# Attention by 128-token tile over all heads, woven into a SwiGLU feed-forward block

## The chip, the cores and the metric

The kernel runs on one core of one Trainium2 chip. The metric is the device time of one execution in microseconds (us). Engines are named as in the profile: PE is TensorE's matrix multiply and PEld its weight load, DVE is VectorE, ACT is ScalarE, POOL is GpSimd and SP is SyncE; POOL and SP issue the DMAs here. L12 is line 12 of the kernel that a row belongs to.

## The reference, cut to what matters

```python
batch, n_heads, seq, head_dim = (8, 8, 576, 64)          # q, k, v, float32
scores = scale * np.matmul(q, k.transpose(0, 1, 3, 2))   # scale = 1/sqrt(64)
bias = slopes[:, None, None] * (-np.abs(rel))            # rel = i - j
mask = (rel >= 0) & (rel < 128)
scores = np.where(mask, scores + bias[None], -1e9)
attn = np.exp(scores - np.max(scores, axis=-1, keepdims=True))
attn = attn / (np.sum(attn, axis=-1, keepdims=True) + 1e-09)
attn_out = np.matmul(attn, v)
x = attn_out.transpose(0, 2, 1, 3).reshape(4608, 512)    # tokens x (heads * head_dim)
g = x @ w_gate                                           # 512 x 1536
out = (g / (1 + np.exp(-g)) * (x @ w_val)) @ w_out       # 1536 x 512
```

Each query sees itself and the 127 keys before it. Both kernels compute exp(score) without the maximum and multiply by a constant table of exp(bias), which is 0 outside the window, and get the sum of the weights as a 65th column of ones beside v.

## The kernel before, in words

The kernel holds x transposed, in four fp16 tiles `xT` of 128 channels by 4608 tokens (L83). It walks through the 8 batches (L187) and in each through 4 pairs of heads (L192).

For a pair of heads, SP issues nine DMAs in rows of 256 bytes that bring q, k and v in fp32 (L199, L203). PE transposes q and k in fp32 with an identity (L216, L218), and ACT copies the results to fp16 `qT` and `kT` (L221, L222) and v to `va` (L227, L229). PE makes the scores with keys on the output partitions (L247; the two heads use the upper and the lower 64 rows of the array), ACT applies Exp (L255 to L259), and DVE multiplies by the table (L264 to L267). The weighted sum (L279 to L285) has v as the stationary operand, so that its result has the head's 64 channels and the row of sums on the output partitions and the queries along the free axis. ACT copies the 64 rows to `avs` (L290, L291), and DVE copies the one row of sums to `cs` (L293, L295).

The division for a whole batch is in `batch_tail` (L165): two reciprocals of 128x576 (L168, L169), a matmul per head that spreads the reciprocal over 64 partitions (L176, L178), and multiplications that write `xT` (L180, L182). It is called after the first pair of heads of the next batch (L301).

The feed-forward block, `moe_block` (L125), takes 512 tokens at a time. For each of 12 column blocks of the hidden layer it runs 4 gate matmuls (`pg_`, L133) and 4 value matmuls (`pv_`, L138) of 128x512, then a Tanh on ACT (`tt`, L143) and two operations on DVE (`uu`, L145; `hT`, L148). The three PSUM banks of the tag "gv" go round. Then come 4 output tiles of 12 matmuls each (`po_`, L152) in one PSUM bank, a copy on ACT (`osb`, L156) and an output DMA from POOL (L157). There are nine such blocks and 1296 matmuls in them. A block is called at the third pair of heads of a batch (L303), and the last two after all of the attention (L312). A scheduler in the tile framework moves instructions within each engine's queue, so that attention and feed-forward matmuls come mixed around these calls; within a queue the order is then fixed.

The weights come through POOL's queue in fp32 in twelve DMAs, and ACT casts them to fp16 (L97 to L108), called after the first pair of heads.

Of the kernel before, what the change touches and what calls it, by code (L numbers as in the profile page):

```python
# [12 lines left out]
ALU = mybir.AluOpType  # L14


@with_exitstack
def kernel(
# [10 lines left out]
    nc = tc.nc  # L29

# [3 lines left out]
    WIN = 128  # L34
    P = 128

    NQT = (S + P - 1) // P
    LAST = S - (NQT - 1) * P
    HP = H // 2
    NKB = DM // P  # L40
    NMB = DFF // P
    NNB = NTOK // 512
    BCOL = 512

    slopes = [2.0 ** (-8.0 * (hh + 1) / H) for hh in range(H)]

    jj = np.arange(P)[:, None]
    ii = np.arange(P)[None, :]
    bconst = np.zeros((P, H, 2, P), dtype=np.float32)
    for hh in range(H):  # L50
        for dq in range(2):
            u = ii - jj + 128 * dq
            valid = (u >= 0) & (u < WIN)
            bconst[:, hh, dq, :] = np.where(valid, np.exp(-slopes[hh] * u), 0.0)
    b0 = bconst[:, :, 0, :]
    b1 = bconst[:, :, 1, :]
    tmask = np.concatenate([b0, b1], axis=2).astype(np.float16)
    tmask2 = np.concatenate(
        [b0, b1[:, :, 0:64], b0[:, :, 0:64]], axis=2).astype(np.float16)
    ident32 = np.eye(P, dtype=np.float32)  # L60
    ident16 = np.eye(P, dtype=np.float16)

    sel = np.zeros((P, 4, 64), dtype=np.float16)
    for j in range(4):
        sel[32 * j, j, :] = 1.0

    tmask_d = nc.inline_tensor(tmask, name="tmask")
    tmask2_d = nc.inline_tensor(tmask2, name="tmask2")
    ident32_d = nc.inline_tensor(ident32, name="ident32")
    sel_d = nc.inline_tensor(sel, name="selconst")  # L70

    consts = ctx.enter_context(tc.tile_pool(name="consts", bufs=1))
    idm = consts.tile([P, P], FP32, name="idm")
    nc.sync.dma_start(idm, ident32_d.ap())
    tm = consts.tile([P, H, 256], FP16, name="tm")
    nc.sync.dma_start(tm, tmask_d.ap())
    tm2 = consts.tile([P, H, 256], FP16, name="tm2")
    nc.sync.dma_start(tm2, tmask2_d.ap())
    selc = consts.tile([P, 4, 64], FP16, name="selc")
    nc.sync.dma_start(selc, sel_d.ap())  # L80

    xt_pool = ctx.enter_context(tc.tile_pool(name="xt", bufs=1))
    xT = [xt_pool.tile([P, NTOK], FP16, name=f"xT{pg}", tag=f"xT{pg}")  # L83
          for pg in range(NKB)]

# [259 lines left out]
```

## Time and profile before

| What | Value |
|---|---|
| Median of the 3 runs (lowest, highest) | 566.29 us (565.98, 566.87) |
| Span of the profiled execution, first to last instruction | 566.0 us |
| Mean granted TensorE clock over the span | 0.927 |
| Instructions in the span | 7238 |
| DMA packets and bytes | 120676, 48.84 MB |

The profile shows one execution. For this one the page gives the span and no time of its own beside it; the runs stand between 0.0 and 0.9 us off the span. A row of a group of instructions reads: line, engine, operation, output<-inputs, shapes, count | busy us, mean ns of one | idle time of that engine just before them and what ended it. A row of the timeline or of the chain of waits begins with its start in us and its length; a matmul's length covers its way through the array, so that the next one starts earlier than it ends. A row of the table by stretches gives, for each engine, busy us and the count of instructions, then the granted clock as a share of full speed, the DMA engines' busy share, and GB/s.

### The profile page before, as it was taken

The numbers are of one execution on the slowest core, as the hardware profiler recorded it, in microseconds if no ns is written. First come the engines' busy times: TensorE is split into PE (matmuls) and PEld (weight loads), VectorE is DVE, ScalarE is ACT, GpSimd is POOL, SyncE is SP. The second block draws the span as 40 slices with busy tenths as digits, with TensorE's granted clock in tenths as the row PEclk, the third lists the DMA queues.
The fourth block names the chain that finished last, engine by engine and source line by source line (L and its number), as shares of the span: only waits on it lengthen the run. The fifth ranks groups of instructions, "written<-read, shape, count | busy, mean of one in ns | idle before, by whom it ended". The sixth has DMA issues, their size and how long they took to land.

```text
span 566.0 us, 7238 instructions
## 1 busy us (share of the span) xinstructions
PE 469.6 (83%) x2448; PEld 237.9 (42%) x2448; DVE 366.0 (65%) x720; ACT 277.4 (49%) x669; POOL 27.3 (5%) x52
## 2 busy tenths in 40 slices
PE   1634689986999699969996999789986999599994
PEld 0322435443544355434544354445443544144441
DVE  1222778759774967497758786678758774875450
ACT  3868718352844466455645383528353844032321
POOL 1110000010001000100000000100010001000001
PEclk9999999996999699978998699969996999699998
DMA  8997614132412423142414241424131101000101
GB/s 262 309 300 212 139 28 112 41 112 67 104 44 76 104 62 86 59 102 62 104 52 107 51 106 26 122 51 100 42 101 38 43 1 57 19 2 19 57 11 63
DMA packets 120676, 48.84 MB, mean 86 GB/s; under 512 B 116032, under 2 KB 116288, under 8 KB 120640
## 3 DMA queue, kind: packets, MB, share of 16 engines
q1 hardware_dynamic: 115776, 29.51, 23.6%
q0 software_dynamic: 4864, 18.88, 9.4%
q8 instruction: 19, 0.31, 0.2%
q14 instruction: 17, 0.14, 0.1%
HBM read 38.93 MB, written 9.44 MB: 85 GB/s over the span
## 4 chain that ended last, share of the span: by engine, by line
PE 41%; issue 30%; DVE 13%; ACT 7%; DMA 7%; POOL 1%; POOLq 0%; ACTq 0%
PE pt_a L216 3%; DVE rc L168 3%; DMA wtmp<-in_moe_w_gate_dram 3%; PE bcA L176 3%; DVE cs L293 2%; DMA wtmp<-in_moe_w_val_dram 2%; PE avA L279 2%; DMA wtmp<-in_moe_w_out_dram 2%; ACT osb L156 2%; DVE ex L264 2%; DVE xT L180 1%; POOL out_dram L157 1%; DVE cs L190 1%; PE pt_b L218 1%; ACT exr L255 1%
## 5 line engine op out<-in xcount | busy, mean ns | idle before, releaser
L264 DVE TENSOR_TENSOR ex<-exr,tm 128x768 f16<-128x768 f16 x64 | 34.9, 545 | 85.0 <-ACT exr L257 84.3
L279 PE MATMUL avA<-ex,va 128*65 128x256 f16 (+1 forms) x256 | 44.7, 304 | 35.4 <-DVE ex L264 31.1
L152 PEld LDWEIGHTS <-hT 128*128 128x128 f16 x432 | 42.1, 98 | 51.5 <-issue 4.3
L138 PEld LDWEIGHTS <-wv_sb 128*128 128x128 f16 x432 | 42.5, 98 | 49.9 <-issue 4.1
L133 PEld LDWEIGHTS <-wg_sb 128*128 128x128 f16 x432 | 41.1, 99 | 52.8 <-issue 13.7
L293 DVE COPY cs<-avA 1x512 f32<-1x512 f32 x64 | 43.4, 678 | 17.5 <-ACT avs L290 16.8
L180 DVE TENSOR_TENSOR xT<-avs,bcA 64x512 f16<-64x512 f16 x64 | 43.5, 680 | 13.0 <-PE bcB L178 11.5
L279 PEld LDWEIGHTS <-va 128*65 128x65 f16 x256 | 30.6, 126 | 49.0 <-issue 37.3
L221 ACT ACTIVATE qT<-pt_a 128x512 f16<-128x512 f32 x32 | 19.1, 597 | 64.6 <-PE pt_a L216 64.6
L290 ACT CAST avs<-avA 64x512 f16<-64x512 f32 x64 | 37.0, 578 | 25.1 <-PE avB L283 23.5
L176 PE MATMUL bcA<-rc,selc 128*64 128x512 f16 x64 | 34.6, 568 | 16.4 <-DVE cs L293 5.7
L157 POOL DMA_DIRECT2D out_dram<-osb x36 | 19.5, 542 | 493.9 <-ACT kT L222 357.5
L247 PE MATMUL ps<-qT,kT 64*128 64x256 f16 (+2 forms) x320 | 31.6, 274 | 7.4 <-ACT kT L221 7.4
L255 ACT ACTIVATE exr<-ps 128x512 f16<-128x512 f32 x64 | 34.8, 598 | 6.0 <-PE ps L247 5.4
L257 ACT ACTIVATE exr<-ps 128x448 f16<-128x448 f32 x64 | 34.3, 545 | 0.0
L216 PE MATMUL pt_a<-idm,qnat 128*128 128x128 f32 x128 | 22.1, 300 | 14.6 <-DMA knat<-in_k_dram 12.7
L168 DVE RECIPROCAL rc<-cs 128x576 f16<-128x576 f32 x8 | 30.0, 3753 | 0.3
L169 DVE RECIPROCAL rc<-cs 128x576 f16<-128x576 f32 x8 | 29.9, 3738 | 0.3
L216 PE MATMUL pt_a<-idm,knat 128*128 128x128 f32 x128 | 22.9, 306 | 5.6 <-ACT qT L221 5.6
L247 PEld LDWEIGHTS <-kT 64*128 64x128 f16 (+1 forms) x320 | 15.0, 100 | 27.4 <-ACT kT L221 12.7
L216 PEld LDWEIGHTS pt_a<-idm,qnat 128*128 128x128 f32 x128 | 16.5, 152 | 19.5 <-DMA knat<-in_k_dram 12.7
L176 PEld LDWEIGHTS <-selc 128*64 128x64 f16 x64 | 9.4, 148 | 28.9 <-issue 20.9
(647 smaller groups left out, 878.2 us busy)
## 6 DMA issues: line engine op xcount, KB each, us to landing
out_dram<-osb POOLq DMA_DIRECT2D x36, 256.0 KB, 2.3
qnat<-in_q_dram SPq DMA_DIRECT2D x64, 128.0 KB, 2.7
knat<-in_k_dram SPq DMA_DIRECT2D x64, 128.0 KB, 2.9
vnat<-in_v_dram SPq DMA_DIRECT2D x64, 128.0 KB, 2.6
wtmp<-in_moe_w_gate_dram POOLq DMA_DIRECT2D x4, 768.0 KB, 6.7
wtmp<-in_moe_w_val_dram POOLq DMA_DIRECT2D x4, 768.0 KB, 6.6
wtmp<-in_moe_w_out_dram POOLq DMA_DIRECT2D x4, 768.0 KB, 6.2
tm<-tmask SPq DMA_DIRECT2D x2, 512.0 KB, 5.8
```

What stands on the lines that cost most here:

```text
L133: nc.tensor.matmul(pg_, wg_sb[:, kb, m * P:(m + 1) * P], xT[kb][:, col0:col0 + ncol], start=(kb == 0), stop=(kb == NKB - 1))
L138: nc.tensor.matmul(pv_, wv_sb[:, kb, m * P:(m + 1) * P], xT[kb][:, col0:col0 + ncol], start=(kb == 0), stop=(kb == NKB - 1))
L152: nc.tensor.matmul(po_, hT[:, m, mb * P:(mb + 1) * P], wo_sb[:, m, :], start=(m == 0), stop=(m == NMB - 1))
L168: nc.vector.reciprocal(rc[:, 0, :], cs[:, 0, :])
L176: nc.tensor.matmul(bcA, selc[:, j_, :], rc[:, g_, 0:512], start=True, stop=True)
L180: nc.vector.tensor_mul(xT[hp][hb:hb + 64, c0:c0 + 512], avs[:, 0:512], bcA)
L216: nc.tensor.transpose(pt_a[:, t * P:(t + 1) * P], src[:, t, :, :], idm)
L247: nc.tensor.matmul(pss[hh][0:kr, c0:c0 + w], kT[hb:hb + 64, kt * P:kt * P + kr], qT[hb:hb + 64, qc:qc + w], start=(si == 0), stop=(si == l ...
L255: nc.scalar.activation(exr[hh][:, 0:512], ps, AF.Exp)
L264: nc.vector.tensor_mul(ex[hh][:, 0:768], exr[hh][:, 0:768], tmr)
L279: nc.tensor.matmul(avA[:, ac:ac + w], va[:, kt, hh, :], ex[hh][:, ec:ec + w], start=(si == 0), stop=(si == 3))
L293: nc.vector.tensor_copy(cs[32 * j_:32 * j_ + 1, g_, 0:512], avA[64:65, :])
```

## The change

The attention is written anew; the arithmetic of the feed-forward block stays. Batches are taken in pairs. A pair has 9 tiles of 128 tokens: 4 of the first batch, 4 of the second, and one that holds the last 64 tokens of both. A tile with all 8 heads is a unit, and there are 36 units.

- Loads: POOL issues one DMA each for q, k and v of a tile, again in rows of 256 bytes, and the DMA casts fp32 to fp16 on its way into SBUF (L143). The weights come the same way, straight into their fp16 tiles (L344, L404), without ACT. The output DMAs move from POOL to SP (L328). SP loads four tables instead of two.
- Transposes: 8 fp16 transposes of 128x128 per tile go to one PSUM bank, and DVE copies them out (L162 to L166).
- Scores: as before with keys on the output partitions, the two heads of a pair on the two halves of the array's rows; 8 matmuls of 256 columns per unit (L209), 4 Exps of 128x512 on ACT with the scale in them (L223), 2 multiplications of 128x1024 by the table on DVE (L227).
- Weighted sum: the weights are the stationary operand and v with its column of ones the moving one (65 columns), so that queries are on the output partitions: 16 matmuls per unit (8 or 24 at the ends, L254). The sum is then a column, and the division is a reciprocal of 128x4 and a multiplication of 128x256 on DVE, twice per unit (L256, L257). `batch_tail` with its spreading matmuls, and the copies `avs` and `cs`, go.
- Since x now has tokens on partitions, 4 more transposes per unit and a copy on ACT make the feed-forward block's operand (L281, L282).
- Order: attention and feed-forward are generators. The feed-forward one yields after every 4 matmuls; a loop at the end of the program draws from both, about one step of attention for one of feed-forward, a unit being 8 steps. An output tile of block n-1 is run in three steps after each of the column blocks 1 to 4 of block n. The last four output tiles use the four banks of the attention.

In the diff, `att_step()` draws one step of the attention.

```diff
-    def batch_tail(args):
...
+    def load(rank):
...
+        for t_, src in ((tk, k), (tq, q), (tv, v)):
+            for p0, p1, b, r0 in pieces(s, c):
+                nc.gpsimd.dma_start(
+                    t_[p0:p1, :, 0:D],
+                    src[b, :, r0:r0 + p1 - p0, :].rearrange("h p d -> p h d"))
...
+        pt = ps_a.tile([P, 8, P], FP16, name="pt", tag="a")
+        for j in range(4):
+            nc.tensor.transpose(pt[:, j, :], tk[:, 2 * j:2 * j + 2, :], idm)
+        for j in range(4):
+            nc.tensor.transpose(pt[:, 4 + j, :], tq[:, 2 * j:2 * j + 2, :], idm)
+        nc.vector.tensor_copy(kTs[s][:, :, cols], pt[:, 0:4, :])
+        nc.vector.tensor_copy(qTs[s][:, :, cols], pt[:, 4:8, :])
...
+            for n, (j, w, val) in enumerate(todo):
+                nc.tensor.matmul(av[:, j, :], w, val, start=(n == 0), stop=(n == len(todo) - 1))
+            rec = xpool.tile([P, 4, 1], FP32, name="rec", tag="rec", bufs=4)
+            nc.vector.reciprocal(rec, av[:, :, D:D + 1])
+            nc.vector.tensor_mul(x[:, 4 * half:4 * half + 4, :], av[:, :, 0:D],
+                                 rec.broadcast_to([P, 4, D]))
...
+        for kb in range(NKB):
+            nc.tensor.transpose(pt[:, kb, :], x[:, kb * P:(kb + 1) * P], idm)
+        nc.scalar.copy(dst, pt)
...
+    def attention():
...
+            if i < last:
+                transposes_to(need_rank[i + 1])
+                after = scores(i + 1)
+            for n in range(4):
+                for f in after[n]:
+                    f()
+                if n == 2 and i + 2 <= last:
+                    transposes_to(need_rank[i + 2])
+                yield i
+            weighted(i)
+            yield i
+            loads_to(i + 8)
+            yield i
+            x_transposed(i)
+            yield i
+            yield i + 1
...
+    load_w(wg2, wg_sb, 0, 128)
+    load_w(wv2, wv_sb, 0, 128)
+    loads_to(3)
...
+    for a0 in (0, 6):
+        nc.gpsimd.dma_start(wo_sb[:, a0:a0 + 6, :], wo2[:, a0:a0 + 6, :])
+    loads_to(7)
...
+        target = base + step * (4.55 * 8) / per_block
+        while att_done < target and att_step():
+            att_done += 1
```

POOL's queue at the start of the program, before: `wtmp` is the fp32 buffer that ACT casts from.

```order
L340 UNCONDITIONAL_BRANCH
L101 DMA wtmp<-in_moe_w_gate_dram 128x1536
L101 DMA wtmp<-in_moe_w_val_dram 128x1536
L104 DMA wtmp<-in_moe_w_out_dram 128x3x512
L101 DMA wtmp<-in_moe_w_gate_dram 128x1536
```

The same queue at a later place of its first part, now: `kn`, `qn` and `va` are the k, q and v of a tile.

```order
L344 DMA wv_sb<-in_moe_w_val_dram 128x4x512
L140 MEMSET va 128x8
L143 DMA kn<-in_k_dram 128x8x64
L143 DMA qn<-in_q_dram 128x8x64
L143 DMA va<-in_v_dram 128x8x64
L404 DMA wo_sb<-in_moe_w_out_dram 128x6x512 x2
L140 MEMSET va 128x8
L143 DMA kn<-in_k_dram 128x8x64
```

POOL's queue held the weights alone, beside SP's with q, k and v; now all of them stand in one queue, and the tiles 6 and 7 (the last of the first eight) behind all of the weights.

PE's queue where the first feed-forward matmul stands, before, with buffer numbers: `bcA` and `bcB` spread the reciprocals of batch 0, and `pg__852` is the first gate tile.

```order
L176 LDWEIGHTS selc_64
L176 MATMUL bcA_637<-rc_116,selc_64 64x512
L178 LDWEIGHTS selc_64
L178 MATMUL bcB_638<-rc_116,selc_64 64x64
L133 LDWEIGHTS wg_sb_76
L133 MATMUL pg__852<-xT0_69,wg_sb_76 128x512
```

The same place now: `px_502` are the transposes of the fourth unit's x, and `ps_524` and `ps_525` the last scores of the sixth unit.

```order
L281 LDWEIGHTS x_470
L281 MATMUL px_502<-idm_58,x_470 128x128
...
L209 LDWEIGHTS kT_174
L209 MATMUL ps_519<-qT_173,kT_174 128x256
...
L209 MATMUL ps_524<-qT_173,kT_174 128x256
...
L209 MATMUL ps_525<-qT_173,kT_174 128x256
...
L295 LDWEIGHTS wg_sb_65
L295 MATMUL pg_509<-xT_283,wg_sb_65 128x512
```

In front of this first gate matmul now stand 64 transposes of q and k (those of tiles 0 to 7), 48 score matmuls (units 0 to 5), 56 of the weighted sum and 16 of x; behind it stand the 1296 feed-forward matmuls with 224, 272, 488 and 128 of these four kinds between them.

DVE's queue in the first feed-forward block, before:

```order
L145 SCALAR_TENSOR_TENSOR uu<-tt,pg__897 128x512
L293 COPY cs<-avA 1x512
L295 COPY cs<-avB 1x64
L293 COPY cs<-avA 1x512
L295 COPY cs<-avB 1x64
L148 TENSOR_TENSOR hT<-uu,pv__898 128x512
L145 SCALAR_TENSOR_TENSOR uu<-tt,pg__912 128x512
```

DVE's queue in a stretch of gate and value steps, now:

```order
L227 TENSOR_TENSOR ex<-exr,m_reg 128x1024 x2
L300 SCALAR_TENSOR_TENSOR uu<-tt,pg 128x512
L256 RECIPROCAL rec<-av 128x4
L310 TENSOR_TENSOR hT<-uu,pv 128x512
L257 TENSOR_TENSOR x<-av,rec 128x256
L256 RECIPROCAL rec<-av 128x4
L257 TENSOR_TENSOR x<-av,rec 128x256
L300 SCALAR_TENSOR_TENSOR uu<-tt,pg 128x512
```

Before, a head pair's copies of the sums stood between `uu` and `hT`; now a unit's reciprocals and multiplications do, and its multiplications by the table ahead of them, all through the program.

More of the change, by code (lines that the diff above doesn't have):

```diff
@@ L55 @@
[L55 to L68, printed above, removed]
@@ L80 @@
[L80 to L84, printed above, removed]
[L86 to L90 removed]
+    NSUP = B // 2
```

522 lines of the change are left out of this document (294 added, 228 removed).

## The prediction

> **What bounds the kernel now.** I read the page's busy shares first, then its chain of work that ended last, then that chain in order of time, and then the places that it names in the table by stretches and in the timeline.
>
> ```profile
> span 566.0 us, 7238 instructions
> PE 469.6 (83%) x2448; PEld 237.9 (42%) x2448; DVE 366.0 (65%) x720; ACT 277.4 (49%) x669; POOL 27.3 (5%) x52
> PE 41%; issue 30%; DVE 13%; ACT 7%; DMA 7%; POOL 1%; POOLq 0%; ACTq 0%
> ```
>
> PE leads, alone or with its issue for 71% of the chain, but DVE, ACT and DMA hold 27%. A busy 83% says little, since each matmul is counted with its way through the array; what a matmul costs is the step from one start to the next, in the chain in order of time:
>
> ```profile
> 100.63 0.86 PE pg__942 L133 x4
> 109.26 0.86 PE pg__1017 L133 x4
> 131.76 1.02 DVE cs L190
> 190.85 1.02 DVE cs L190
> ```
>
> Ten groups of 4 matmuls lie between the first two rows, 8.63 us: 0.863 a group, with nothing between. The feed-forward part has 1296/4 = 324 groups, 280 us. The last two rows are one point of two successive batches, 59.1 us apart. A block of feed-forward is 36 groups, 31.1 us, so a batch pays 28 us beside it, for attention and waits. The waits show in the timeline:
>
> ```profile
> 185.52 3.74 DVE L169 RECIPROCAL rc<-cs 128x576 f16<-128x576 f32 x1
> 189.72 0.91 PE L279 MATMUL avA<-ex,va 128*65 128x256 f16 x4 [3.39 <-DVE ex L264]
> 195.86 0.63 PE L138 MATMUL pv__2185<-xT,wv_sb 128*128 128x512 f16 x1
> 196.28 0.63 PE L133 MATMUL pg__2199<-xT,wg_sb 128*128 128x512 f16 x1
> 200.68 0.38 PE L138 MATMUL pv__2185<-xT,wv_sb 128*128 128x512 f16 x1
> 200.89 0.38 PE L133 MATMUL pg__2199<-xT,wg_sb 128*128 128x512 f16 x1
> 550.14 2.75 PE L152 MATMUL po__5676<-wo_sb,hT 128*128 128x512 f16 x12 [0.67 <-ACT osb L156]
> ```
>
> Once a batch a reciprocal of 576 columns holds DVE's queue, the multiplication by the table stands behind it, and PE sits 3.39 us. The clock then falls: at 196 us matmuls start 0.42 apart, at 200.7 again 0.21. Each output tile also waits 0.67 for its one bank. The first 50 us belong to the DMAs:
>
> ```profile
> 0.00:10.00 10.00, 0.00 (x0) 0.00 (x0) 2.18 (x5) 2.14 (x2) 1.42 (x6) 1.00 0.80 285
> 10.00:20.00 10.00, 4.01 (x20) 2.43 (x21) 0.22 (x1) 7.37 (x14) 1.86 (x3) 1.00 1.02 276
> 20.00:30.00 10.00, 6.32 (x32) 4.08 (x32) 2.97 (x11) 7.73 (x15) 1.34 (x2) 1.00 1.19 291
> 30.00:40.00 10.00, 4.31 (x20) 3.14 (x20) 3.45 (x11) 7.74 (x17) 1.86 (x3) 1.00 1.15 309
> 40.00:50.00 10.00, 4.13 (x24) 2.45 (x23) 1.46 (x5) 5.99 (x10) 1.29 (x2) 1.00 1.07 284
> ```
>
> They are fully busy and move 289 GB/s on average (last column).
>
> **The change part by part.** The new time is a sum along PE: the start until the first gate matmul, then all that PE's queue holds behind it, its waits, and the end.
>
> *Start.* PE's queue puts the transposes of tiles 0 to 7 ahead of the first gate matmul, and POOL's queue puts tiles 6 and 7 behind all weights. So 8 tiles of 3 x 0.262 MB, 9.44 MB of weights and 1.84 MB of tables must land: 17.6 MB, at 289 GB/s 61 us. With the last landing (about 3) and transposes, copies and scores behind it, 66 us. What a casting DMA costs no row shows: if only the bytes written counted, 9.7 MB, the start is 26 us shorter; at half the rate, 61 us longer. I take the read bytes, since rows of 256 bytes are what q, k and v are read in now.
>
> *Clock.* PE is mostly idle in the start, so the first matmuls run as at 196 us: half speed lasted there from the end of the 3.39 us wait (189.72) until shortly before 200.68, 11 us, and half of that, 5 us, is lost. By the Trainium skill, TensorE: Matmul & The Clock Gate, Part 1: The HAM clock gate, about 3.4 us of sustained work release the clock, which would lose 1.7 and make the sum 3 less; the trace's 11 us disagrees.
>
> *Feed-forward.* The same 324 groups, 280 us. The 0.67 before an output tile goes, since other steps stand between.
>
> *Attention on PE.*
>
> ```profile
> 203.39 0.84 PE L247 MATMUL ps<-qT,kT 64*128 64x256 f16 x10
> 205.98 0.54 PE L279 MATMUL avA<-ex,va 128*65 128x256 f16 x4
> 206.31 0.11 PEld L283 LDWEIGHTS <-va 128*65 128x65 f16 x1
> 206.36 0.19 PE L283 MATMUL avB<-ex,va 128*65 128x64 f16 x1
> 206.48 0.21 PE L285 MATMUL avB<-ex,va 64*65 64x64 f16 x1
> 206.63 0.39 PE L133 MATMUL pg__2214<-xT,wg_sb 128*128 128x512 f16 x1
> L133 PEld LDWEIGHTS <-wg_sb 128*128 128x128 f16 x432 | 41.1, 99 | 52.8 <-issue 13.7
> ```
>
> Ten score matmuls of 960 columns per head took 0.84 us, their way out of the array included; the 8 of a unit have 1024 columns per head. Without the last way out (0.2) I take 0.63; 30 units behind the start make 19 us. The new weighted sums (488) and transposes (224 + 128) are 840 matmuls of 65 or 128 columns, each with a load of 128 columns. The rows of the old weighted sum bound one: 896 columns passed from 205.98 to 206.36, so 128 take 0.054 and 65 take 0.028; the short ones stepped by 0.12 and 0.15; a load not hidden at all (0.099) before 65 columns makes 0.127. The load at 206.31 had its matmul start 0.05 later, so I take 0.06: 840 x 0.06 = 50 us (34 to 107).
>
> *DVE*, which feeds PE:
>
> ```profile
> L293 DVE COPY cs<-avA 1x512 f32<-1x512 f32 x64 | 43.4, 678 | 17.5 <-ACT avs L290 16.8
> L264 DVE TENSOR_TENSOR ex<-exr,tm 128x768 f16<-128x768 f16 x64 | 34.9, 545 | 85.0 <-ACT exr L257 84.3
> L265 DVE TENSOR_TENSOR ex<-exr,tm 128x192 f16<-128x192 f16 x64 | 15.8, 247 | 0.0
> L180 DVE TENSOR_TENSOR xT<-avs,bcA 64x512 f16<-64x512 f16 x64 | 43.5, 680 | 13.0 <-PE bcB L178 11.5
> L182 DVE TENSOR_TENSOR xT<-avs,bcB 64x64 f16<-64x64 f16 x64 | 13.1, 205 | 0.0
> L295 DVE COPY cs<-avB 1x64 f32<-1x64 f32 x64 | 13.4, 210 | 0.0
> 543.23 0.69 DVE L145 SCALAR_TENSOR_TENSOR uu<-tt,pg__5615 128x512 f16<-128x512 f16 x1 [0.25 <-ACT tt L143]
> 543.26 1.03 PE L133 MATMUL pg__5630<-xT,wg_sb 128*128 128x512 f16 x4
> 544.02 0.69 DVE L148 TENSOR_TENSOR hT<-uu,pv__5616 128x512 f16<-128x512 f16 x1
> 544.12 1.03 PE L138 MATMUL pv__5631<-xT,wv_sb 128*128 128x512 f16 x4
> ```
>
> A unit needs two copies out of PSUM (0.678 each by L293), two table products of 1024 columns (0.68, by the slope between L265 and L264), two reciprocals of 4 columns (0.2, by the short copy L295) and two products of 256 columns (0.41, between L182 and L180): 3.94 us, against 2.3 of PE (19 + 50 over 30). A gate and value pair needs 1.38 of DVE in 1.73 of PE, and there DVE idles 0.25, and a little more: the bank that 544.12 fills had been freed at 543.92, the end of the row at 543.23. So where 4 pairs stand in a unit's 8 steps, at most 1.0 of the extra 1.64 is covered, and 0.6 is not; the wait of x's transposes for two reciprocals and two products (1.2, behind a 0.69) against two steps (1.73) adds some 0.2. Rounded up, 0.9 for each of 30 units: 27 us (0 to 60). What PE, ACT and DVE did in `batch_tail`, and its 3.39 us waits, go with it; ACT has 4 Exps, a copy and 4 Tanhs of 0.6 in 10 us and is not late. By the Trainium skill, VectorE: DVE Perf Modes, The perf-mode tier table, a 16-bit copy out of PSUM may run at twice the rate; by its cycle table for such copies one is an estimated 0.39, and the 27 would be about 10. No row here has a 16-bit source in PSUM.
>
> *Loads later.* A tile (0.786 MB) each 11 us or so is a quarter of 289 GB/s, four tiles ahead in buffers; nothing. Output DMAs move to SP, which otherwise holds only tables: nothing.
>
> *End.*
>
> ```profile
> 559.82 0.58 ACT L156 COPY osb<-po__5708 128x512 f32<-128x512 f32 x1 [2.88 <-PE po__5708 L152]
> ```
>
> From this last copy to the span's end (566.0) are 6 us, and they stay.
>
> Sum: 66 + 5 + 280 + 19 + 50 + 27 + 6 = **453 us**, made against the span of 566.0; the runs' median, 566.29, differs by less than my rounding.
>
> **The rivals.** *DVE sets the pace.* In the 16 of 36 steps of a block that hold gate and value pairs only, all of DVE's 3.94 us would show, not 0.9: 13 units x 3.04 = 40 more, 493 us. For it: the slack of 0.2 to 0.25 in the rows above, smaller than any new operation but one. Against: PE's attention matmuls run meanwhile. 15%.
>
> *Casting DMAs run at half rate.* The start is 127 us, the time 514. Later tiles then take 5.4 us each, still under 11. For it: no row shows a cast. Against: nothing in the rows. 12%.
>
> *POOL cannot write the rows fast enough*, and the kernel is slower.
>
> ```profile
> L101 POOL DMA_DIRECT2D wtmp<-in_moe_w_gate_dram x4: 578/578/673, 1.3 to 38.6; - x4
> L104 POOL DMA_DIRECT2D wtmp<-in_moe_w_out_dram x4: 759/759/759, 10.9 to 47.0; - x4
> ```
>
> A load has 1024 rows where L101's has 128. If all of the 578 ns were per row (4.5 ns), a load takes 4.6 us of POOL, and 108 with the weights' 5632 rows make 523; the last tile's units and two blocks come after, some 80 us (62 for the blocks, 3 units, the end): 603. It is slower than 566 from 4.2 ns a row. Against: L104 has 384 rows and takes 759, 0.7 ns per further row, so 1.2 us a load and 130 in all. 6%. By the Trainium skill, SBUF — State Buffer, Who interferes with whom, VectorE in a two-port mode shuts GpSimd out of writing descriptors, which speaks for this rival; by the same section products of two SBUF inputs and reads of PSUM are no such mode, and the change has no others. No run here shows it.
>
> **How the numbers follow.** The forecast has 66%; 1% is left for no change. Differences of 0.2% are about what this measurement can tell. All but POOL's case and the 1% are faster: 0.93, 0.01, 0.06. The range goes from 410 (cast by written bytes, or no waits and hidden loads) to 515, which takes in the half-rate case and unhidden loads (453 + 57), and leaves POOL's out.
>
> **What would show it.** In the table by stretches, 285 GB/s up to about 61 us and the first gate matmul at 66. In the timeline, matmuls of 65 columns 0.06 apart. In the list of waits, PE's waits for DVE at x and the gate banks near 27 us together. Slow casts show as GB/s near 145 in the first stretch; POOL's limit as a busy POOL throughout. If the first gate matmul comes much off 66, or a unit's 28 short matmuls take over 2.5 us, the sum is wrong.

## The result, and the profile after the change

The changed kernel takes 410.89 us (median of 4 runs, 409.64 to 411.37) against 566.13 of the kernel before on the same chip: a ratio of 0.7258, 95% interval 0.7244 to 0.7272. The forecast was 453 with a range from 410 to 515, so the sign held, and the time came out 42 us below the point. It lies inside the range by 0.9 us only, and that is partly luck: the lower end stood for a start that is 26 us shorter or for no waits, while what happened is that two terms of the sum, the small matmuls and the waits for DVE, were both far too large. The profiled execution has a span of 409.1 us and a granted clock of 0.997, before 0.927. First its page, with the busy shares and the chain that ended last:

```profile
span 409.1 us, 6645 instructions
PE 364.4 (89%) x2592; PEld 181.0 (44%) x2592; DVE 245.9 (60%) x500; ACT 173.8 (42%) x317; POOL 112.0 (27%) x170
PE 73%; DMA 10%; DVE 7%; ACT 5%; issue 2%; POOL 1%; DVEq 0%; POOLq 0%; ACTq 0%
```

PE itself now holds 73% of the chain. What is left of the other engines shows in the list of PE's waits (us in total, times, longest), taken from 62 us to the end:

```profile
PE pv L308 <- DVE uu L300: 1.2, 3, 0.4
PE px L281 <- DVE x L257: 0.7, 3, 0.4
PE po L322 <- ACT osb L326: 0.7, 1, 0.7
```

Behind the start PE waits 2.6 us in all by this list, 1.9 of them for DVE, and never longer than 0.7. The list counts idle time from the end of a matmul's way through the array (0.38 us for 512 columns, where the next one can start after 0.216), so it is a lower count. The steps show more. As a wait I take what a step from one matmul's start to the next has beyond the usual step of that pair, where a semaphore that the second one waits for was updated less than 0.06 us before its start. That is 7.6 us behind the first gate matmul, 4.7 for DVE and 2.5 for ACT. Below, "by the steps" means this count. Over the whole span the same list is led by the loads:

```profile
PE pt L162 <- DMA kn<-in_k_dram: 27.0, 4, 9.4
PE px L281 <- DVE x L257: 5.4, 7, 1.6
```

So what PE waits for lies in the start. That, in the table by stretches (busy us and count of PE, PEld, DVE, ACT and POOL; granted clock, DMA share, GB/s):

```profile
10.00:20.00 10.00, 4.93 (x36) 2.74 (x36) 3.56 (x8) 2.27 (x5) 9.09 (x14) 1.00 2.27 162
20.00:30.00 10.00, 6.94 (x61) 4.17 (x59) 5.76 (x16) 4.61 (x10) 7.59 (x12) 1.00 1.57 191
30.00:40.00 10.00, 1.91 (x13) 0.84 (x13) 1.38 (x2) 2.36 (x5) 4.23 (x8) 1.00 1.54 193
40.00:50.00 10.00, 1.27 (x14) 0.85 (x12) 0.76 (x2) 0.00 (x0) 4.80 (x7) 1.00 1.68 187
```

And its end, in the timeline of PE:

```profile
57.16 0.39 PE L281 MATMUL px<-idm,x 128*128 128x128 f16 x2 [1.12 <-DVE x L257]
59.29 1.89 PE L295 MATMUL pg<-xT,wg_sb 128*128 128x512 f16 x4
60.98 1.48 PE L308 MATMUL pv<-xT,wv_sb 128*128 128x512 f16 x4
62.29 0.39 PE L162 MATMUL pt<-idm,kn 128*128 128x128 f16 x4
```

The DMA engines are busy throughout (shares over 1, where transfers overlap), PE hardly between 30 and 50 us, and the first gate matmul comes at 59.29. The first six steps are 0.40 to 0.43 us, and from 62 us on they are 0.216.

To see where the 157 us between the two profiled executions went, I put each step on PE, from the start of one matmul to the start of the next, to the line of the first one, and summed over all matmuls of a trace (2448 and 2592) from the first feed-forward matmul on. A wait thereby counts to the matmul ahead of it.

| Part of the span, us | before | after | in the forecast |
|---|---|---|---|
| until the first feed-forward matmul | 75.9 | 59.3 | 66 |
| feed-forward steps | 300.3 | 288.2 | 285 (280 + 5 for the clock) |
| attention steps behind it, waits included | 183.2 | 56.3 | 96 (19 + 50 + 27) |
| from the last matmul's start to the end | 6.6 | 5.3 | 6 |
| sum | 566.0 | 409.1 | 453 |

So 127 of the 157 us come out of the attention on PE, 17 out of the start, 12 out of the feed-forward steps and 1 out of the end; the miss of the forecast is 40 us of attention, 7 of start, and 3 the other way.

### The profile page after: what moved, and what is told of

Its sections match the earlier page's. It is cut to its first block, busy times and chain, and to the rows that moved or that the text cites. A ratio compares the mean times of both kernels' runs of the same rounds, so it can differ in the third digit from the quotient of the medians.

```text
span 409.1 us, 6645 instructions
## 1 busy us (share of the span) xinstructions
PE 364.4 (89%) x2592; PEld 181.0 (44%) x2592; DVE 245.9 (60%) x500; ACT 173.8 (42%) x317; POOL 112.0 (27%) x170
## 3 DMA queue, kind: packets, MB, share of 16 engines
q0 software_dynamic: 118304, 18.88, 62.0%
## 4 chain that ended last, share of the span: by engine, by line
PE 73%; DMA 10%; DVE 7%; ACT 5%; issue 2%; POOL 1%; DVEq 0%; POOLq 0%; ACTq 0%
PE po L322 22%; PE pv L308 20%; PE pg L295 20%; DMA kn<-in_k_dram 6%; DMA wv_sb<-in_moe_w_val_dram 4%; ACT exr L223 4%; PE ps L209 3%; PE av L254 3%; PE px L281 3%; DVE uu L300 2%; PE pt L162 1%; PE pt L164 1%; DVE hT L310 1%; DVE exl L227 1%; DVE ex L227 1%
## 5 line engine op out<-in xcount | busy, mean ns | idle before, releaser
L308 PE MATMUL pv<-xT,wv_sb 128*128 128x512 f16 x432 | 112.0, 380 | 1.4 <-DVE uu L300 1.2
L295 PE MATMUL pg<-xT,wg_sb 128*128 128x512 f16 x432 | 112.0, 381 | 0.3
L300 DVE SCALAR_TENSOR_TENSOR uu<-tt,pg 128x512 f16<-128x512 f16 x108 | 73.8, 684 | 61.6 <-ACT tt L298 61.2
L322 PE MATMUL po<-wo_sb,hT 128*128 128x512 f16 x432 | 104.8, 379 | 0.9 <-ACT osb L326 0.7
L298 ACT ACTIVATE tt<-pg 128x512 f16<-128x512 f32 x108 | 65.1, 603 | 79.5 <-PE pg L295 77.6
L223 ACT ACTIVATE exr<-ps 128x512 f16<-128x512 f32 x128 | 67.4, 608 | 39.7 <-PE ps L209 39.7
L310 DVE TENSOR_TENSOR hT<-uu,pv 128x512 f16<-128x512 f16 x108 | 74.0, 685 | 8.3 <-PE ps L209 1.0
L143 POOL DMA_DIRECT2D kn<-in_k_dram x40 | 34.0, 853 | 113.3 <-PE pt L164 101.9
L227 DVE TENSOR_TENSOR ex<-exr,m_reg 128x1024 f16<-128x1024 f16 x48 | 33.1, 689 | 36.2 <-ACT exr L223 36.2
L282 ACT COPY xT<-px 128x512 f16<-128x512 f16 x36 | 21.0, 584 | 50.9 <-PE px L281 50.8
L162 PE MATMUL pt<-idm,kn 128*128 128x128 f16 x144 | 15.7, 238 | 27.9 <-DMA kn<-in_k_dram 27.0
L143 POOL DMA_DIRECT2D va<-in_v_dram x40 | 33.8, 851 | 7.3 <-POOL va L140 5.0
L143 POOL DMA_DIRECT2D qn<-in_q_dram x40 | 34.1, 854 | 5.1 <-DMA wo_sb<-in_moe_w_out_dram 2.9
L257 DVE TENSOR_TENSOR x<-av,rec 128x256 f16<-128x256 f32 x72 | 29.0, 419 | 0.7
L209 PE MATMUL ps<-qT,kT 64*128 64x256 f16 (+1 forms) x288 | 27.2, 282 | 2.3 <-DVE qT L166 2.3
L162 PEld LDWEIGHTS <-kn 128*128 128x128 f16 x144 | 11.1, 105 | 35.4 <-DMA kn<-in_k_dram 29.1
L281 PE MATMUL px<-idm,x 128*128 128x128 f16 x144 | 18.8, 230 | 5.5 <-DVE x L257 5.4
```

Of the source, the lines that this page charges most:

```text
L143: nc.gpsimd.dma_start(t_[p0:p1, :, 0:D], src[b, :, r0:r0 + p1 - p0, :].rearrange("h p d -> p h d"))
L162: nc.tensor.transpose(pt[:, j, :], tk[:, 2 * j:2 * j + 2, :], idm)
L209: nc.tensor.matmul(two[par][:, j, o:o + w], kT[rows, pair, kcols], qT[rows, pair, cols], start=(j == 0 and n == 0), stop=(j == 1 and n == ...
L223: nc.scalar.activation(er[:, o:o + 2, :], banks[q4][par], AF.Exp, scale=scale)
L227: nc.vector.tensor_mul(e[:, o, :], er[:, o, :], m[:, o, :])
L281: nc.tensor.transpose(pt[:, kb, :], x[:, kb * P:(kb + 1) * P], idm)
```

## The experiments

Two questions were open: why the waits and the short matmuls cost so much less than the sum had them, and which of the old kernel's faults the 157 us were. All times are medians of 4 runs; "slower" is against the changed kernel's 410.9, and the kernel before ran beside each (565.9 to 566.2).

### Is there room on DVE?

```diff
-        nc.vector.tensor_copy(kTs[s][:, :, cols], pt[:, 0:4, :])
-        nc.vector.tensor_copy(qTs[s][:, :, cols], pt[:, 4:8, :])
+        for _ in range(2):                      # 4 in the second kernel
+            nc.vector.tensor_copy(kTs[s][:, :, cols], pt[:, 0:4, :])
+            nc.vector.tensor_copy(qTs[s][:, :, cols], pt[:, 4:8, :])
```

> The changed kernel with each copy of transposed queries and keys out of PSUM issued twice: 72 more VectorE instructions of about 0.42 us, some 0.34 apart, so about 25 us more work on VectorE and none on TensorE. Theory A (VectorE's steps overlap and it has room in every stage, so the 27 us of waits that the prediction charged for it are not there): less than 5 us slower than 410.9. Rival B (VectorE is close to setting the pace, and the waits were small only by a little): 15 to 25 us slower, as waits of TensorE for the copies and for x.

Measured: 418.4, 7.5 slower.

> The same copies issued four times: 216 more VectorE instructions, some 73 us of steps, so that VectorE would be busy for about 320 of the 409 us. Theory A (room on VectorE in every stage): 5 to 20 us slower, since the copies stand in bursts that the PSUM banks only partly cover. Rival B (VectorE at the edge): 60 to 75 us slower, the whole of what is added.

Measured: 445.2, 34 slower. The granted clock reads 0.949 in the profiled execution, but 0.949 to 0.984 in the four runs at times from 443.8 to 445.5, and 15 of the 23 us that 0.949 stands for are one stretch of half clock in the start (36.6 to 67.3 us), so it does not explain the time. What an operation costs, by the group of the copies and by three rows of DVE's timeline, both of the changed kernel:

```profile
L165 DVE COPY kT<-pt 128x512 f16<-128x512 f16 x36 | 15.1, 418 | 31.6 <-PE pt L164 31.4
```

```profile
330.39 0.18 DVE L256 RECIPROCAL rec<-av 128x4 f32<-128x4 f32 x1
330.50 0.69 DVE L310 TENSOR_TENSOR hT<-uu,pv 128x512 f16<-128x512 f16 x1
331.11 0.42 DVE L257 TENSOR_TENSOR x<-av,rec 128x256 f16<-128x256 f32 x1
```

A copy takes 0.418, not 0.678, and an operation that waits for nothing starts before the one ahead of it ends: 0.61 behind the start of a product that takes 0.69, 0.33 behind that of a copy (median of the steps).

Both theories missed in their pure form: 30% of 25 us shows, and 47% of 73. DVE has room, but not without end. The first kernel gives a unit nearly the price that the forecast had charged for its copies (4 steps of 0.33 against 2 x 0.678), so that error alone was worth at most 7.5 of the 22 us by which the waits were overcharged (27 against 4.7 by the steps).

### What does a short matmul cost?

```diff
+            todo = [one for one in todo for _ in range(2)]
             for n, (j, w, val) in enumerate(todo):
```

> The changed kernel with each weighted-sum matmul (65 columns) issued twice, so that numerator and sum both double and their quotient stays: 544 more matmuls of that kind on TensorE, nothing elsewhere. Theory A (behind the first gate matmul TensorE is the path, and one such matmul costs the 0.029 to 0.036 us that the trace shows from start to start): 16 to 20 us slower than 410.9. Rival B (the price in the prediction, 0.06 us each): 33 us slower. Rival C (TensorE waits for others behind such matmuls anyway): below 5 us.

Measured: 420.5, 9.6 slower, so below every number of theory A, and far below B. By line, the steps of the weighted sums rose from 17.4 us for 488 to 31.3 for 976, 13.9 or 0.0285 each; feed-forward steps fell by 2.5 (1.0 because the first gate matmuls ran at full speed here, 1.0 because their waits are shorter, 0.5 not traced further), the start by 0.5. The timeline of the changed kernel shows such a row of them:

```profile
329.70 0.19 PE L254 MATMUL av<-va,ex 128*128 128x65 f16 x1
329.73 0.20 PE L254 MATMUL av<-va,exl 128*128 128x65 f16 x1
...
330.15 0.20 PE L254 MATMUL av<-va,exl 128*128 128x65 f16 x1
330.19 1.46 PE L322 MATMUL po<-wo_sb,hT 128*128 128x512 f16 x6
```

Sixteen matmuls in 0.49 us, 0.030 each: nothing of the load of 128 columns ahead of each shows. TensorE is the path here (C is out), and the price is the time of the columns alone, the lower bound that the forecast had (0.028) and did not take.

### What is the order worth?

Three kernels undo one thing each in how the work is mixed. Output tiles in one piece at the end of their block, out of one bank:

```diff
-                if n > 0 and 1 <= m <= 4:
-                    yield from project(n - 1, m - 1, ps_f, "po", 1)
-        for j in range(4):
-            yield from project(NBLK - 1, j, ps_a, "a", 4)
+            for j in range(4):
+                for _ in project(n, j, ps_f, "po", 1):
+                    pass
+            yield
...
-    per_block = 24 + 12
+    per_block = 24 + 1
...
-        blk = 0 if step < 24 else 1 + (step - 24) // per_block
+        blk = step // per_block
```

(The last two changes fit the loop that draws the steps to a block of 25.)

> The changed kernel with the output projection put back as it stood before the change: the four output tiles of a block run in one piece behind the block's last hidden product, out of one PSUM bank, with no attention or gate matmul between them. Theory A (the splitting and delaying of the projections removed a wait for ScalarE's eviction of about 0.67 us per output tile, 36 of them, and the wait for the last hidden product once a block): 20 to 35 us slower than 410.9, as waits of TensorE for osb at the first matmul of a tile. Rival B (the evictions are hidden either way): within 5 us.

Measured: 418.4, 7.5 slower. PE's waits for the eviction are only 2.3 us in the list:

```profile
PE po L322 <- ACT osb L326: 2.3, 4, 0.7
```

They are 1.6 more than in the changed kernel; by the steps they are 5.6 us against 1.3, so more than half of the 7.5. The wait of theory A exists, but at about a fifth of the least size that it gave. With that falls the forecast's sentence that each output tile waits 0.67: the scheduler puts gate, score and weighted-sum matmuls between the output tiles, here as in the kernel before, whose list has this wait just three times, at the last three tiles:

```profile
PE po__5692 L152 <- ACT osb L156: 0.7, 1, 0.7
PE po__5708 L152 <- ACT osb L156: 0.7, 1, 0.7
PE po__5676 L152 <- ACT osb L156: 0.7, 1, 0.7
```

No mixing of attention and feed-forward in the program (the scheduler still moves some output-tile matmuls between attention steps):

```diff
-        while att_done < target and att_step():
+        while blk >= NBLK and att_step():
```

> The changed kernel with the same instructions but without the mixing: ahead of each feed-forward block all attention steps that it needs are issued in one stretch, and the block then runs alone. Theory A (the mixing covers the waits of a unit for ScalarE's exponentials and VectorE's products; a unit alone takes about as long as ScalarE and VectorE need for it, 2.4 to 2.7 us, against some 1.6 us of TensorE work): 35 to 60 us slower than 410.9, more if the granted clock falls in these stretches. Rival B (only the sum of TensorE's instructions counts, as the bound of the prediction with no waits has it): less than 10 us slower.

Measured: 434.4, 23.5 slower: between the two. The attention steps grow from 56.3 to 75.0 us, the feed-forward steps from 288.2 to 293.9. The waits behind the start are 10.7 us in the list, 8 more than with mixing (19.7 by the steps, 12 more):

```profile
PE po L322 <- ACT osb L326: 6.2, 9, 0.7
PE px L281 <- DVE x L257: 3.8, 7, 0.7
```

Two banks in place of three for gate and value:

```diff
-    ps_f = ctx.enter_context(tc.tile_pool(name="ps_f", bufs=3, space=PSUM))
+    ps_f = ctx.enter_context(tc.tile_pool(name="ps_f", bufs=2, space=PSUM))
```

> The changed kernel with two PSUM banks for gate and value results in place of three (one bank stays unused). Theory A (the third bank is what lets TensorE run on past tanh, sum and product of 0.60, 0.68 and 0.69 us; with two, the gate matmul of the next step waits for the bank of this one): 20 to 80 us slower than 410.9, as waits of TensorE at pg and pv. Rival B (attention matmuls between the steps cover these evictions anyway): less than 5 us slower.

Measured: 422.9, 12 slower, less than theory A and more than rival B. The list has only 3.4 us of waits at the gate bank. By the steps PE waits 11.2 us for `uu`, whose end frees that bank, against 2.4 in the changed kernel: 8.8 of the 12. So the mechanism of theory A holds, at about half of its least size.

In all three kernels a part of what is lost lies at the scores. In an unbroken row the two matmuls of a pair of heads start 0.004 us apart and the next pair 0.11 later; the last one of a row takes 0.20, so that the 8 of a unit take 0.54 us. A matmul of 512 columns right ahead of a row takes 0.312 where 0.216 is usual. Where the scheduler puts other matmuls between the scores, a unit pays this for several rows: there are 41 rows behind the first gate matmul in the changed kernel, and 52, 72 and 58 in these three. The steps of L209 sum to 4.1, 7.8 and 4.8 us more than in the changed kernel; of the 4.8 (two banks) more than half are waits.

### Is the start DMA time?

```diff
+    loads_to(7)                                # kernel 1: wo behind tiles 6 and 7
     for a0 in (0, 6):
         nc.gpsimd.dma_start(wo_sb[:, a0:a0 + 6, :], wo2[:, a0:a0 + 6, :])
-    loads_to(7)
```

> The changed kernel with the load of wo issued behind the loads of token tiles 6 and 7 instead of ahead of them; the same bytes and instructions. Theory A (the 59 us ahead of the first gate matmul are the DMA engines' time for tiles and weights in the order of issue, and tile 6 lands behind wo's 1.5 MB): first gate matmul at about 49 us, 8 to 12 us faster than 410.9. Rival B (the start is set by the attention chain of the first units, or POOL's issuing): within 3 us.

Measured: 403.8, 7.1 faster, a little less than theory A; first gate matmul at 51.16, not 49.

The second moves the weights' columns beyond 512 behind tiles 7 and 8 too, and wo to the last place:

```diff
-    loads_to(3)
+    loads_to(4)
+    load_mask("lo")
     load_w(wg2, wg_sb, 128, 512)
     load_w(wv2, wv_sb, 128, 512)
-    loads_to(4)
-    load_mask("lo")
-    for c0 in (512, 1024):
-        load_w(wg2, wg_sb, c0, c0 + 512)
-        load_w(wv2, wv_sb, c0, c0 + 512)
-    loads_to(5)
+    loads_to(7)
+    load_w(wg2, wg_sb, 512, 1024)
+    load_w(wv2, wv_sb, 512, 1024)
+    loads_to(8)
+    load_w(wg2, wg_sb, 1024, 1536)
+    load_w(wv2, wv_sb, 1024, 1536)
+    loads_to(9)
...
-    loads_to(7)
```

> The changed kernel with its loads reordered: token tiles 0 to 7 first, of the gate and value weights only the first 512 columns ahead of tiles 4 to 7, the other columns between tiles 8 and 9, wo last. Theory A (the start is DMA time in the order of issue; about 4.5 MB of the 9.4 go behind the first gate matmul): first gate matmul at about 35 us, 18 to 25 us faster than 410.9, unless the later columns then come late. Rival B (the start is set by the attention chain of the first block's four units): within 5 us. Rival C (the gate and value columns come too late, and the stall only moves): the first gate matmul early, but gaps at L295 and L308 of 10 us or more in the first block.

Measured: 394.3, 16.6 faster, a little less than theory A; first gate matmul at 42.64, not 35. Behind it the sum of the steps is 344.6 us as against 344.5 in the changed kernel: nothing is given back.

The third changes the order on PE as well, so that the scores of unit 4 come behind x of unit 3, and draws the attention faster in the first block (`load_gv` loads the columns of wg and wv, `ahead` holds the scores of the next unit and the transposes of the one behind it):

```diff
...
+    loads_to(2)
+    load_mask("lo", nc.gpsimd)
+    load_gv(0, 256)
+    loads_to(6)
+    load_gv(256, 512)
+    load_gv(512, 1024)
+    loads_to(7)
...
         for i in range(last + 1):
+            if i != 3:
+                yield from ahead(i, i)
             weighted(i)
...
+            if i == 3:
+                yield from ahead(i, i + 1)
```

> The changed kernel with a start of its own: tiles 0 to 2, 256 columns of the gate and value weights, tiles 3 to 6, then the other columns, tiles 7 and 8 and wo; the tables lo, hi and com on GpSimd's queue where they are needed, and the scores of unit 4 behind x of unit 3, so that fewer steps stand ahead of the first gate matmul. Theory A (the start is the DMA engines' time for the bytes ahead of the first gate matmul, here 5.5 MB of tiles, 1.0 of weights and 1.0 of tables at about 290 GB/s, 26 us, and 4 for the last chain): first gate matmul at about 30 us, 27 to 31 us faster than 410.9. Rival B (the weight columns then come too late and the stall moves into the first block): first gate matmul near 30, but only 15 to 20 us faster. Rival C (the chain of the first four units through ScalarE and VectorE holds the start): first gate matmul not before 38.

Measured: 389.9, 21.0 faster and the fastest of all (ratio to the kernel before 0.6888, interval 0.6878 to 0.6899). Between the theories: the first gate matmul comes at 35.06, not 30, and 3 us are lost again in the first block. Its timeline on PE:

```profile
18.61 0.60 PE L162 MATMUL pt<-idm,kn 128*128 128x128 f16 x4 [2.72 <-DMA kn<-in_k_dram]
...
22.05 0.40 PE L281 MATMUL px<-idm,x 128*128 128x128 f16 x2 [1.78 <-DVE x L257]
...
27.22 0.39 PE L281 MATMUL px<-idm,x 128*128 128x128 f16 x2 [1.12 <-DVE x L257]
...
31.18 0.39 PE L281 MATMUL px<-idm,x 128*128 128x128 f16 x2 [0.76 <-DVE x L257]
...
35.06 1.02 PE L295 MATMUL pg<-xT,wg_sb 128*128 128x512 f16 x4
...
48.33 0.61 PE L162 MATMUL pt<-idm,kn 128*128 128x128 f16 x4 [4.59 <-DMA kn<-in_k_dram]
```

From 22 us on the units follow each other 4 to 5 us apart with waits for DVE's x and small matmuls at half speed: the chain of the first units holds the start now, as rival C has it, though earlier than it said. And tile 7's keys come 4.59 late, since they stand behind weight columns.

### What were the old kernel's faults?

In the kernel before, the reciprocals replaced (the softmax division is left out):

```diff
-            nc.vector.reciprocal(rc[:, 0, :], cs[:, 0, :])
-            nc.vector.reciprocal(rc[:, 1, :], cs[:, 1, :])
+            nc.vector.tensor_copy(rc[:, 0, :], cs[:, 0, :])
+            nc.vector.tensor_copy(rc[:, 1, :], cs[:, 1, :])
```

> The kernel before the change with its two reciprocals of 576 columns a batch replaced by copies of the same tile; this leaves the softmax division out. Theory A (each batch's 7.5 us of reciprocals holds VectorE's queue, TensorE then idles 3.4 us and runs at half clock for 10 to 14 us behind it, seven times): 45 to 65 us faster than 566, the granted clock near 1 in place of 0.927. Rival B (TensorE's waits there come from the rest of the chain through ScalarE and VectorE and stay): at most 10 us faster, the clock as before.

Measured: 547.0, ratio 0.9673 (0.9648 to 0.9699), 18.9 faster, clock 0.941. Both theories miss. Against the copies (0.46 us each, where a reciprocal took 3.74) the reciprocals cost about 2.4 us a batch. The 3.39 us wait shrinks to 1.75, but the low clock stays, as PE's timeline at the same place shows:

```profile
181.67 0.91 PE L279 MATMUL avA<-ex,va 128*65 128x256 f16 x4 [1.75 <-DVE ex L264]
...
185.09 0.58 PE L176 MATMUL bcA<-rc,selc 128*64 128x512 f16 x1 [0.49 <-DVE cs L293]
185.94 0.59 PE L176 MATMUL bcA<-rc,selc 128*64 128x512 f16 x1 [0.21 <-DVE xT L180]
186.78 0.59 PE L176 MATMUL bcA<-rc,selc 128*64 128x512 f16 x1 [0.20 <-DVE xT L180]
...
190.67 0.58 PE L133 MATMUL pg__2199<-xT,wg_sb 128*128 128x512 f16 x1
191.18 0.40 PE L176 MATMUL bcA<-rc,selc 128*64 128x512 f16 x1
```

What remains is a chain in which PE, ACT and DVE wait for each other: scores, Exp and table product of the next pair, then the spreading matmuls, each of which waits for DVE's products of the one before.

One part of the change alone, in the kernel before:

```diff
-idm = consts.tile([P, P], FP32, name="idm")
+idm = consts.tile([P, P], FP16, name="idm")
...
-                t_ = qkv_nat.tile([P, NQT, 2, D], FP32, name=name + "nat",
+                t_ = qkv_nat.tile([P, NQT, 2, D], FP16, name=name + "nat",
...
-                    nc.sync.dma_start(
+                    nc.gpsimd.dma_start(
...
-                pt_a = psum.tile([P, 512], FP32, name="pt_a", tag=PSTAG)
+                pt_a = psum.tile([P, 512], FP16, name="pt_a", tag=PSTAG)
```

> The kernel before the change with one part of the change alone: q, k and v are loaded by casting DMAs of GpSimd as 16-bit numbers, and the transposes of q and k are 16-bit, identity and PSUM tile included; all else as before. Theory A (a fp32 transpose of 128 columns steps by 0.109 us and a 16-bit one by 0.056, so the 320 transposes and what they wait for cost half): 15 to 30 us faster than 566. Rival B (the reciprocals' stall and the layout of the attention hold the time, and shorter transposes only wait longer): within 5 us. Rival C (casting loads of 128-byte rows feed the start too slowly): slower, with the first feed-forward matmul later than before.

Measured: 561.2, ratio 0.9913 (0.9886 to 0.9941), 4.8 faster: rival B. The transposes of full tiles (L216) fell from 29.5 to 17.9 us of steps behind the first feed-forward matmul, but the first one came 2.8 us later, and the steps of L218, behind which PE waits for ACT, rose by 2.7.

And the stall put into the changed kernel, twice 3.75 us on DVE for each batch:

```diff
+            if half == 0 and p in (0, 4):
+                for _ in range(2):
...
+                        nc.vector.reciprocal(
+                            rc, av[:, 0, D:D + 1].broadcast_to([P, 576]))
             nc.vector.reciprocal(rec, av[:, :, D:D + 1])
```

> The changed kernel with two reciprocals of 576 columns put on VectorE's queue once a batch behind the first weighted sum of the batch's first tile (their result isn't read), as the kernel before had them; eight times, the first in the start. Theory A (a block of 7.5 us on VectorE makes TensorE idle for some 3 us and then lowers the clock for 10 to 14 us, whatever the layout of the rest): 50 to 65 us slower than 410.9, granted clock near 0.9. Rival B (the mixing with the feed-forward work and the four output tiles covers the block): 0 to 20 us slower, the clock near 1.

Measured: 440.8, 29.9 slower, clock 0.974 (0.965 to 0.974 in the four runs): between the theories. Its added operations in the groups of lines, PE's largest wait behind the start, and the timeline of one stall:

```profile
L260 DVE RECIPROCAL rc<-av 128x576 f16<-128x576 f32 x16 | 60.0, 3749 | 0.9 <-PE av L255 0.9
```

```profile
PE px L287 <- DVE x L263: 11.5, 8, 2.9
```

```profile
125.15 0.40 PE L287 MATMUL px<-idm,x 128*128 128x128 f16 x2 [2.27 <-DVE x L263]
...
130.07 1.87 PE L314 MATMUL pv<-xT,wv_sb 128*128 128x512 f16 x4
131.78 0.65 PE L255 MATMUL av<-va,ex 128*128 128x65 f16 x16
```

PE's waits behind the start are 15.9 us in the list, 13.3 more than in the changed kernel, and 22.8 by the steps, 15.2 more: about half of the 28.6 by which the spans differ. The clock lost is at most (1 - 0.974) x 437.7 = 11.4 us against 1.2, since PE is idle in part of that time. It is lost at three of the eight places, for 6.8 us each (from 70.3, 125.0 and 299.0 us on), and in the last 2 us. So the mixing does not make the kernel immune: half of the 60 us put on DVE shows in the time.

## Why the forecast was 42 us too long

**Start, 66 forecast, 59.3 measured.** The cause was right: moving 3.1 MB of wo behind the tiles brought the first gate matmul 8.1 us forward, and moving 7.3 MB 16.7. Two sizes were off, in opposite directions. The last awaited keys landed at 49 us, not 61: the chain in order of time has

```profile
33.44 15.54 DMA kn<-in_k_dram
```

and the column GB/s counts written bytes, half of what a casting DMA reads (all of POOL's queue is 18.88 MB, for 37.7 MB of inputs), so that 183 GB/s between 10 and 50 us are 367 GB/s read, against the 289 that I took from rows without a cast. Behind the landing, the chain of the last unit took 10 us, not 5. (Two side cases are slightly off by the forecast's own numbers: written bytes alone would save 27 us, not 26, and half the rate for the 15.7 MB that are cast would add 54, not 61.)

**Clock, 5 forecast.** The first gate matmuls ran at half speed for 2.5 us, 1.3 lost; the feed-forward steps were 288.2 rather than 285, because another 7 us stand over 0.216 a step: 3.9 of waits by the steps, and 3.5 where matmuls of different kinds follow each other. (That each output tile of the old kernel waits 0.67 was wrong, as shown above; the sum held nothing for it.) My reading of the 11 us was wrong: I counted from the end of the 3.39 us wait, but PE went idle again and again behind it. In the kernel before:

```profile
192.46 0.58 PE L176 MATMUL bcA<-rc,selc 128*64 128x512 f16 x1 [0.46 <-DVE cs L293]
...
194.05 0.58 PE L176 MATMUL bcA<-rc,selc 128*64 128x512 f16 x1 [0.21 <-DVE xT L180]
...
194.89 0.58 PE L176 MATMUL bcA<-rc,selc 128*64 128x512 f16 x1 [0.20 <-DVE xT L180]
...
200.25 0.26 PE L178 MATMUL bcB<-rc,selc 128*64 128x64 f16 x1
200.44 0.40 PE L133 MATMUL pg__2184<-xT,wg_sb 128*128 128x512 f16 x1
```

Full speed came 5.6 us after the last idle time; in the changed kernel 4.7 after the wait that ended at 57.16, with two copied reciprocals about 4.2 after 186.78, with the stall put in about 6 after 125.15. The rule of the Trainium skill, TensorE: Matmul & The Clock Gate, Part 1: The HAM clock gate, that sustained work of about 3.4 us releases the clock, is nearer to these 4 to 6 us than my 11; the 3 us that the sum would have been less by it were right.

**Small matmuls, 50 forecast.** This term failed. With the medians of the steps (0.029 for 65 columns, 0.056 for 128) the 840 cost 33.9 us (38.2 with the waits and changes of kind behind them), at the lower bound of 34, whose own prices of 0.028 and 0.054 make 33; the step of the argument that failed is "the load at 206.31 had its matmul start 0.05 later, so I take 0.06": that was latency, not the distance between two matmuls. Doubling the weighted sums confirmed 0.0285.

**Scores, 19 forecast.** Their steps sum to 18.1, so the term was right, though its own rows give a little more (0.64 us for 960 columns is 0.68 for 1024, not 0.63). At 0.052 for 256 columns, half of what a pair takes in an unbroken row, it would be 13.4; the rest is the ends of the rows and 1 us of waits.

**Waits for DVE, 27 forecast.** This term failed outright: 4.7 us by the steps and 1.9 in the list, near the lower bound of 0. (The attention steps have 56.3 - 33.9 - 13.4 = 9.0 us over these prices: 3.7 of waits for DVE and ACT, the rest where one kind of matmul follows another, a cost that the forecast lacked.) The mechanism exists, since extra work on DVE shows by a third to a half. The size was off for two reasons. The durations: steps of 0.33 for a copy, 0.61 for a table product, 0.11 and 0.34 for reciprocal and x add to 2.8 us a unit, not 3.94, since an operation that waits for nothing starts before the one ahead of it ends. The copies alone were worth at most 7.5 us, as measured. By the Trainium skill, VectorE: DVE Perf Modes, The perf-mode tier table, a copy of 16-bit data out of PSUM can run at twice the rate. The trace agrees: the forecast's estimate of 0.39, from the cycle table of that page, was nearly right (0.418). The rest I had charged by following the steps of the program one by one ("at most 1.0 of the extra 1.64 is covered", "the wait of x's transposes ... against two steps"), while the scheduler moves other matmuls into such places: even without mixing in the program, PE waited 3.8 us for x by the list, 5.8 by the steps. How the rest divides between the two was not isolated.

**End, 6 forecast, 5.3 measured.** Loads of later tiles and output DMAs were hidden, as said: no such wait stands in the list behind the first block.

**The rivals.** DVE did not set the pace: of 25 us more work, 7.5 showed. Casting DMAs didn't halve the rate of what is read. POOL took 0.853 us a load, where the forecast had 1.2 and the rival 4.6:

```profile
L143 POOL DMA_DIRECT2D kn<-in_k_dram x40 | 34.0, 853 | 113.3 <-PE pt L164 101.9
```

**Where the gain came from.** 157 us are 17 of start, 12 of feed-forward steps, 127 of attention steps and 1 of the end. Alone, the reciprocals were worth 19 and the fp16 loads and transposes 5. The clock was worth at most 40 ((1 - 0.927) x 566 = 41, less 1.2), part of it inside the 19. Behind the first feed-forward matmul PE's waits fell from 45 us to 2.6 in the list and from some 60 to 7.6 by the steps, so about a third of the gain are waits that are gone; of these the mixing covers at most 23.5, what the kernel without it loses. The other steps on PE simply no longer exist (bcA and bcB had 41.6 us behind the first feed-forward matmul, waits included). How much of the gain is the layout with queries on the partitions and how much the pipelining of units, these runs don't separate: neither was put into the old kernel alone.

## What to carry to other kernels

Price an instruction by the distance to the next one where it stands in a row of its kind, on DVE as on PE; a duration or the delay behind a weight load is latency and overcharges by up to a factor of two. Then add what a change of kind costs (here about 0.1 us on each side of a row of scores), and count waits by these steps, since a list of idle times misses the short ones. A removed stall gives back little when the next chain stands right behind it, so look at what ends second before giving it a price (19 us of an expected 45 to 65). When a start is DMA time, order the loads by who needs them first: here the order alone was worth 16.6 us on top of the change.

## What the runs showed of the hardware that I had not expected

- Full clock came only 4 to 6 us after PE's last idle time, and idle times of 0.2 to 0.5 us put it off: in the kernel before they stretched half speed to 10 to 14 us. Waits of 1.75 and 2.27 us sufficed for the drop; the longest of the changed kernel behind its start (0.7) had none. But one wait's length does not decide: with the stall put in, waits of 2.27 us that end at 125.15 and 299.27 us came with half clock, and one of 2.28 that ends at 214.17 did not; in the kernel without mixing, half clock stands from 177.6 to 181.0 us at a wait of 0.70. That the small gaps prolong it is read from four traces, not tested by itself.
- In the start of the changed kernel the granted clock reads 1.00 while matmuls step at half speed (0.427 at 59.7 to 61.8 us); there only the steps tell. For the same reason the mean over the span is a poor measure: in the four runs with every copy issued twice it reads 0.961 to 0.998, at times from 417.7 to 419.0.
- Packets of a casting DMA took 34 ns each, those of 256 bytes without a cast 18.5, and yet the loads went at 367 GB/s read. From the queues of the kernels after and before (packets, MB, share of 16 engines' span: 62.0% of 16 x 409.1 us over 118304, and 23.6% of 16 x 566.0 over 115776):

```profile
q0 software_dynamic: 118304, 18.88, 62.0%
```

```profile
q1 hardware_dynamic: 115776, 29.51, 23.6%
```

- A matmul of 65 columns with a weight load of 128 columns of its own steps by 0.029 us; the load is hidden wholly.
- Score matmuls of 256 columns on the two halves of the rows start 0.004 us apart, and a pair takes 0.11. Each break in a row of them costs about 0.2 more: the last one of a row takes 0.20, and the 512-column matmul ahead of the next row 0.312 in place of 0.216.
